# Second batch of a fused attention and SwiGLU kernel: its last q and weight transposes moved from TensorE to DMA, and the third batch's loads and projection moved to fit

## Chip, cores, metric

One NeuronCore of a Trainium2 chip. The metric is device time in microseconds (us) of one execution, median of several. Each changed kernel is timed in the same rounds as the kernel before. A ratio and its 95% interval are from fast runs alone; they are not quite the ratio of the medians quoted beside them. A second measure is used below, the *stream*: from the first TensorE transpose of slot 12 (at 33.8 to 35.2 us, before any TensorE work that the change touches) to the end of the profiled execution. That slot is reached up to 1.4 us earlier or later from run to run, and the stream leaves that out. Each stream is that of one profiled execution.

## The reference

Attention with keys and values projected from 1024 rows to 64 (Linformer), eight batches of eight heads, then a SwiGLU block over all 8192 tokens:

```python
k_proj = einsum('ks,bhsd->bhkd', E, k);  v_proj = einsum('ks,bhsd->bhkd', F, v)
attn = softmax(q @ k_proj.T / sqrt(64));  x = attn @ v_proj       # per batch and head
g = x @ w_gate;  out = (silu(g) * (x @ w_val)) @ w_out            # 512 -> 1536 -> 512
```

## The kernel before

The SwiGLU matmuls of 16 half batches (12 steps each, t = 0 to 191) form one long stream on TensorE. In a step, the g matmuls multiply by `w_gate`, the v matmuls by `w_val`, the y matmuls by `w_out`. Attention for the next batch is cut into small units and dropped into numbered slots of that stream: slot 2t follows the g matmuls of step t, slot 2t+1 follows its v and y matmuls. Elsewhere v is the values of attention, and a *turn* is a transpose of q or of the attention weights, by TensorE or by DMA; the prediction also calls a step a turn. Batches are counted from b = 0, so b = 1 is "the second batch".

```python
BY_DMA = [(b, ch) for b in range(1, B) for ch in range(CH)][1:]   # all but (1, 0)

def load_k(b, ...):  nc.gpsimd.dma_start(out=kb[b]..., in_=k[b]...)   # fp32 -> bf16, from GpSimd's queue
# load_v, load_q(b, ch): the same

def u_KV(b, what="kv"):      # projection: 8 x (k matmul, v matmul), side by side in the array
    for j in range(NJ):
        for _, lo, w, src in todo: nc.tensor.matmul(...)              # L147
    ...                      # evictions, k on ScalarE, v on VectorE

def u_T(b, u):               # turn of q on TensorE: 4 transposes, 1 eviction
def u_A(b, u):               # turn of the attention weights on TensorE: 4 transposes, 1 eviction
def u_TD(b, ch):             # turn of a half batch of q by DMA, from SyncE's queue
    nc.sync.dma_start_transpose(out=t[:], in_=qb[b, ch]...)
def u_AD(b, ch):             # turn of a half batch of weights by DMA, same queue (also used by the stores)
    nc.sync.dma_start_transpose(out=t[:]..., in_=AA.pop((b, ch, "d"))...)

def u_S(b, u): ...           # score: 4 matmuls (L227), exp on ScalarE
def u_R(b, u): ...           # row sum and reciprocal on VectorE
def u_N(b, u): ...           # multiply on GpSimd (L258)
def u_PV(b, ch, pr): ...     # weights x values (L285), eviction to xT, which the SwiGLU matmuls read
```

GpSimd issues the loads and does the multiplies in one queue, in order; SyncE issues DMA turns and stores in one queue, in order.

The softmax here doesn't subtract the row's maximum and nothing guards it: scores larger than these inputs give would overflow.

## Time and profile before

| | kernel before |
|---|---|
| time, median (range) | 573.73 us (572.9 to 574.41, 4 runs) |
| profiled span | 572.4 us |
| TensorE busy | 561.2 us, 98% |
| stream (slot 12 to the end) | 537.75 us |
| TensorE waits after 26 us | none |

Here is the top of the list of TensorE's waits (who waited for whom: us in total, times, longest), all of them in the first 26 us while the first inputs come in:

```profile
PE kvp L147 <- DMA kb<-in_k_dram: 1.3, 2, 1.0
PE warm L458 <- DVE zeros L434: 1.2, 1, 1.2
PE kvp L147 <- DMA vb<-in_v_dram: 1.0, 2, 0.6
```

### The profile page before, as it was taken

The page shows a single profiled execution, that of the slowest core. Times are in us where ns is not written, and L with a number is a line of the kernel's source. Part 1 is how long each engine was busy: PE and PEld are TensorE (multiplying, and loading weights), DVE is VectorE, ACT ScalarE, POOL GpSimd, SP SyncE. Part 2 cuts the span into 40 slices and gives each one's busy share as a digit, 9 for nine tenths or more (in the row PEclk, how much of TensorE's full clock was granted, in tenths as well). Part 3 has the DMA queues.
Part 4 walks back from the last instruction along what each step waited for, and adds up shares of the span by engine and source line. Part 5 has one row for each costly group of instructions (what it writes and reads, how often), then busy time and mean ns, then how long its engine had stood idle before and what let it go on. Part 6 is the DMA issues. An engine that isn't in the chain of part 4 may idle for free.

```text
span 572.4 us, 7867 instructions
## 1 busy us (share of the span) xinstructions
PE 561.2 (98%) x2910; PEld 268.6 (47%) x2967; DVE 336.8 (59%) x580; ACT 237.0 (41%) x416; POOL 107.9 (19%) x121
## 2 busy tenths in 40 slices
PE   8899999999999999999999999999999999999997
PEld 4654544444444444444444444444444444444444
DVE  2787566666466744766556665567546674554550
ACT  1655444353425434444335434354342543443232
POOL 6734131234002400124001330023200220000000
PEclk9999999999999999999999999999999999999999
DMA  9999993539901698037951399204990124100012
GB/s 160 196 200 206 201 161 74 93 64 196 201 37 41 110 190 157 18 75 129 187 108 38 59 179 195 63 22 88 197 176 37 42 52 74 38 37 25 31 39 92
DMA packets 105927, 61.34 MB, mean 107 GB/s; under 512 B 58016, under 2 KB 97696, under 8 KB 105888
## 3 DMA queue, kind: packets, MB, share of 16 engines
q0 software_dynamic: 42288, 29.89, 36.1%
q1 hardware_dynamic: 63312, 30.68, 25.1%
q8 instruction: 23, 0.38, 0.3%
q10 hardware_dynamic: 288, 0.26, 0.1%
q14 instruction: 16, 0.13, 0.1%
HBM read 60.29 MB, written 16.78 MB: 135 GB/s over the span
## 4 chain that ended last, share of the span: by engine, by line
PE 94%; DMA 2%; POOL 1%; ACT 1%; issue 1%; DVE 0%; POOLq 0%
PE yps L360 29%; PE vps L322 29%; PE gps L322 29%; PE kvp L147 3%; PE sc L227 2%; DMA vb<-in_v_dram 2%; PE pv L285 2%; PE aTp L274 0%; ACT xT L135 0%; PE qTp L193 0%; POOL kb L88 0%; PE kTp L172 0%; POOL qb L107 0%; ACT th L334 0%; PE pv L300 0%
## 5 line engine op out<-in xcount | busy, mean ns | idle before, releaser
L341 DVE SCALAR_TENSOR_TENSOR s<-th,gps 128x512 f32<-128x512 f32 x192 | 130.5, 680 | 138.0 <-ACT th L334 137.8
L322 PE MATMUL gps<-xT,wg 128*128 128x512 bf16 (+1 forms) x755 | 195.7, 377 | 1.2
L322 PE MATMUL vps<-xT,wv 128*128 128x512 bf16 (+1 forms) x761 | 195.9, 377 | 0.8
L360 PE MATMUL yps<-wo,hT 128*128 128x512 bf16 (+2 forms) x761 | 191.5, 376 | 0.8
L334 ACT ACTIVATE th<-gps 128x512 f32<-128x512 f32 x192 | 114.6, 597 | 162.6 <-PE gps L322 155.1
L346 DVE TENSOR_TENSOR hT<-s,vps 128x512 bf16<-128x512 f32 x192 | 132.0, 688 | 22.1 <-PE vps L322 1.5
L360 PEld LDWEIGHTS <-hT 128*128 128x128 bf16 x780 | 76.2, 98 | 89.9
L258 POOL TENSOR_TENSOR AAd<-ee,rr 128x512 bf16<-128x512 f32 x52 | 54.1, 1040 | 319.5 <-issue 168.4
L322 PEld LDWEIGHTS <-wv 128*128 128x128 bf16 x776 | 73.9, 98 | 82.9 <-issue 3.3
L322 PEld LDWEIGHTS <-wg 128*128 128x128 bf16 x776 | 74.0, 98 | 81.3 <-issue 0.6
L370 ACT ACTIVATE ysb<-yps 128x512 f32<-128x512 f32 (+1 forms) x65 | 38.4, 590 | 78.1 <-PE yps L360 74.4
L135 ACT CAST xT<-pv 128x512 bf16<-128x512 f32 x62 | 36.1, 585 | 51.3 <-PE pv L285 50.3
L242 DVE TENSOR_REDUCE zz<-ee 128x8 f32<-128x512 f32 x64 | 43.5, 679 | 17.9 <-ACT ee L231 17.9
L231 ACT ACTIVATE ee<-sc 128x512 f32<-128x512 f32 x64 | 37.9, 595 | 17.4 <-PE sc L227 17.4
L285 PE MATMUL pv<-AT,BDV 128*128 128x512 bf16 x60 | 22.6, 379 | 0.1
L227 PEld LDWEIGHTS <-qTd 128*128 128x128 bf16 x208 | 16.0, 98 | 12.3
L227 PE MATMUL sc<-BD,qTd 128*128 128x128 bf16 x208 | 20.1, 219 | 0.1
L135 DVE CAST BDV<-kvp 64x256 bf16<-64x256 f32 x14 | 6.0, 426 | 22.1 <-ACT ks L157 19.1
L258 POOL TENSOR_TENSOR AA<-ee,rr 128x512 bf16<-128x512 f32 x10 | 10.3, 1038 | 35.2 <-DVE rr L244 33.6
L147 PE MATMUL kvp<-kb,ET 128*64 128x512 bf16 (+1 forms) x72 | 15.5, 357 | 1.3 <-DMA kb<-in_k_dram 1.3
L244 DVE RECIPROCAL rr<-zz 128x8 f32<-128x8 f32 x64 | 13.0, 203 | 6.2
L147 PE MATMUL kvp<-vb,FT 128*64 128x512 bf16 (+1 forms) x72 | 15.5, 358 | 1.0 <-DMA vb<-in_v_dram 1.0
(49 smaller groups left out, 144.8 us busy)
## 6 DMA issues: line engine op xcount, KB each, us to landing
out_dram<-ysb SPq DMA_DIRECT2D x63, 256.0 KB, 2.3
qb<-in_q_dram POOLq DMA_DIRECT2D x15, 512.0 KB, 16.6
kb<-in_k_dram POOLq DMA_DIRECT2D x7, 1024.0 KB, 11.6
vb<-in_v_dram POOLq DMA_DIRECT2D x7, 1024.0 KB, 14.2
wo<-in_moe_w_out_dram POOLq DMA_DIRECT2D x2, 768.0 KB, 14.8
wg<-in_moe_w_gate_dram POOLq DMA_DIRECT2D x5, 256.0 KB, 10.4
wv<-in_moe_w_val_dram POOLq DMA_DIRECT2D x5, 256.0 KB, 10.4
kb<-in_k_dram POOLq DMA_DIRECT2D x2, 512.0 KB, 8.7
```

What stands on the lines that cost most here:

```text
L135: (nc.scalar.copy if eng is nc.scalar else eng.tensor_copy)(out=out, in_=in_)
L147: nc.tensor.matmul(out=t[lo : lo + 64, h0:h1].rearrange("p h d -> p (h d)"), lhsT=w[:, j, :], rhs=src[b][:, h0:h1, j, :], start=(j == 0), ...
L227: nc.tensor.matmul(out=ps[:, n, :], lhsT=t[:, n, :], rhs=BD[b % 2][:, 4 * g + n, :], start=True, stop=True)
L231: nc.scalar.activation(out=e[:].rearrange("p h j k -> p (h j k)"), in_=ps[:].rearrange("p a k -> p (a k)"), func=AF.Exp, scale=scale,)
L242: nc.vector.reduce_sum(out=z[:], in_=e[:], axis=AX.X)
L258: eng.tensor_tensor(out=a.rearrange("p j h k -> p h j k"), in0=ee.pop((b, u))[:], in1=rr.pop((b, u))[:].unsqueeze(3).to_broadcast([P, 4, 2 ...
L322: nc.tensor.matmul(out=ps[:, ts], lhsT=(wg, wv)[w][:, kt, f * P : (f + 1) * P], rhs=x[:, kt, ts], start=(kt == 0), stop=(kt == NKT - 1),)
L334: nc.scalar.activation(out=th[:], in_=ps[:], func=AF.Tanh, scale=0.5)
L341: nc.vector.scalar_tensor_tensor(out=s1[:], in0=th[:], scalar=1.0, in1=g[:], op0=ALU.add, op1=ALU.mult)
L346: nc.vector.tensor_tensor(out=hT[c][:, f, :], in0=s1[:], in1=ps[:], op=ALU.mult)
L360: nc.tensor.matmul(out=yy[c][:, cs], lhsT=hT[c][:, f, i * P : (i + 1) * P], rhs=wo[:, f, cs], start=(f == 0), stop=(f == NFT - 1),)
L370: nc.scalar.activation(out=ysb[:, cs], in_=yy[c][:, cs], func=AF.Copy, scale=0.5)
```

## The change

Intent: the half batch (1, 0) is the only one after the first batch whose q and weights are still turned on TensorE. Turn it by DMA like the others. Its q must then be loaded and its k projected earlier, its scores must come at once so that the weights' turn is done in time, and the third batch's loads are put behind all this so that they don't slow the turn. The third batch's projection and scores move to later slots. The diff is cut to its core: equal branches are written out for the batch they serve, old values stand as remarks, and lines without a sign are unchanged.

```diff
-BY_DMA = [(b, ch) for b in range(1, B) for ch in range(CH)][1:]
+BY_DMA = [(b, ch) for b in range(1, B) for ch in range(CH)]
 ... place(b), b == 1:
+            put(22, u_TD, 1, 0)
+            put(29, u_KV, 1, "k")                      # was 34
+            put(32, u_KT, 1)                           # was 36
             put(40, u_KV, 1, "v")
+            sa = (35, 36, 37, 38, 43, 44, 45, 47)      # was (37, 38, 39, 40, 48, 50, 52, 54)
+            put(41, u_AD, 1, 0)
             put(30, u_TD, 1, 1)
+            put(50, u_AD, 1, 1)                        # was 57
+            sp = (44, 45, 46, 46, 66, 67, 68, 69)      # was (43, 44, 45, 46, 66, ...)
-            tt, ta: four u_T and four u_A of (1, 0), slots 35 to 38 and 41 to 44
 ... b == 2 (b > 2 as before):
+            put(s0 + 8, u_KV, b)                       # was s0; s0 = 48
+            put(s0 + 11, u_KT, b)                      # was s0 + 3
+            o = 13                                     # was 14; scores at s0 + o + 3 * j
+            put(s0 + 9, u_TD, b, 0);  put(s0 + 11, u_TD, b, 1)    # were s0 + 3, s0 + 5
 ... load order at the start: weights,
+        load_q(1, 0);  load_k(1)
         load_wo(0);  load_wo(1)                        # q(1, 0) was loaded at slot 20, k(1) after these
 ... loads of the third and fourth batch:
+            at = (46, 47, 48, 48) if b == 2 else ...   # k, v, q, q; were 36, 38, 40, 42
+            s0 = 96 - 20 for b == 3                    # was 96 - 24
```

More of the change, by code (lines that the diff above doesn't have):

```diff
@@ L392, in place @@
         if b == 1:
-            put(30, u_TD, 1, 1)
-            put(34, u_KV, 1, "k")
-            put(36, u_KT, 1)
-            put(40, u_KV, 1, "v")
-            sa = (37, 38, 39, 40, 48, 50, 52, 54)
-            tt = (35, 36, 37, 38)
-            ta = (41, 42, 43, 44)
-            put(57, u_AD, 1, 1)
-            sp = (43, 44, 45, 46, 66, 67, 68, 69)
-        else:
-            put(s0, u_KV, b)
-            put(s0 + 3, u_KT, b)
-            o = 14 if b == 2 else 6
-            put(s0 + (3 if b == 2 else -6), u_TD, b, 0)
-            put(s0 + (5 if b == 2 else -4), u_TD, b, 1)
+            put(22, u_TD, 1, 0)
+            put(29, u_KV, 1, "k")
+            put(32, u_KT, 1)
+            put(40, u_KV, 1, "v")
+            sa = (35, 36, 37, 38, 43, 44, 45, 47)
+            put(41, u_AD, 1, 0)
+            put(30, u_TD, 1, 1)
+            put(50, u_AD, 1, 1)
+            sp = (44, 45, 46, 46, 66, 67, 68, 69)
+        else:
+            put(s0 + (8 if b == 2 else 0), u_KV, b)
+            put(s0 + (11 if b == 2 else 3), u_KT, b)
+            o = 13 if b == 2 else 6
+            put(s0 + (9 if b == 2 else -6), u_TD, b, 0)
+            put(s0 + (11 if b == 2 else -4), u_TD, b, 1)
             sa = [s0 + o + 3 * j for j in range(NJ)]
@@ L412, in place @@
         for j in range(NJ):
-            if (b, j // 4) not in BY_DMA:
-                put(tt[j], u_T, b, j)
-                put(ta[j], u_A, b, j)
             put(sa[j], u_S, b, j)
@@ L507 @@
         load_w_gv(10, 12)
+        load_q(1, 0)
+        load_k(1)
         load_wo(0)
         load_wo(1)
-        load_k(1)
         warm(1)
@@ L532 @@
         put(23, u_PV, 0, 1, 3)
-        put(20, load_q, 1, 0)
         put(20, load_v, 1)
@@ L538 @@
         for b in range(2, B):
-            s0 = 48 * (b - 1) - (12 if b == 2 else 24)
-            put(s0, load_k, b)
-            put(s0 + 2, load_v, b)
-            put(s0 + 4, load_q, b, 0)
-            put(s0 + 6, load_q, b, 1)
+            s0 = 48 * (b - 1) - (20 if b == 3 else 24)
+            at = (46, 47, 48, 48) if b == 2 else (s0, s0 + 2, s0 + 4, s0 + 6)
+            put(at[0], load_k, b)
+            put(at[1], load_v, b)
+            put(at[2], load_q, b, 0)
+            put(at[3], load_q, b, 1)
         for s in slots:
```

## The prediction

> **What bounds the kernel now.** I read the page's first two parts first, then the waits of TensorE, then its timeline around the second batch, then the queues of GpSimd and SyncE over the first 220 us.
>
> ```profile
> PE 561.2 (98%) x2910; PEld 268.6 (47%) x2967; DVE 336.8 (59%) x580; ACT 237.0 (41%) x416; POOL 107.9 (19%) x121
> ...
> PEclk9999999999999999999999999999999999999999
> DMA  9999993539901698037951399204990124100012
> GB/s 160 196 200 206 201 161 74 93 64 196 201 37 41 110 190 157 18 75 129 187 108 38 59 179 195 63 22 88 197 176 37 42 52 74 38 37 25 31 39 92
> ```
>
> TensorE is busy 98% of 572.4 us. Its list of waits holds under 6 us in all, every one before 26 us; asked for 26 to 572 us, the list is empty. So from 26 us on the kernel is one unbroken stream of matmuls, and two rules follow: a matmul taken away shortens the end by its pace, and a new wait of TensorE lengthens it in full, with nothing later to absorb it. The GB/s row (slices of 14.3 us) shows the loads running in plateaus near 200 GB/s with quiet gaps; the three slices from 86 to 129 us are quiet (74, 93, 64 GB/s), because the loads of the third batch (b = 2) lie before them, the last issued at 79.7 us and landed 6.6 us later.
>
> ```profile
> 63.08 0.39 PE L193 MATMUL qTp<-ident_bf,qb 128*128 128x128 bf16 x4
> 63.30 1.03 PE L322 MATMUL gps<-xT,wg 128*128 128x512 bf16 x3
> ```
>
> This is one turn as the change removes it: four transposes of 128 columns start at 63.08 and the next matmul starts at 63.30. A turn costs the stream 0.22 us, 55 ns a transpose; the 219 ns that the source line gives for one is its length in the pipe, not its pace. The four-part turn of the attention weights (L274, 75.77 to 76.00) costs the same.
>
> **What the Trainium skill says.** "TensorE: Matmul & The Clock Gate", section "Back-to-back issue gap", gives about 56 ns for an isolated gap at N = 128 and 81 ns in a stream with weight loads. The trace has 55 ns with weight loads, so I use 55. "DMA: Bandwidth & Descriptors", section "Issuing engines are not separate DMA queues", says that DMAs from SyncE and GpSimd run on the same 16 engines and interleave. The trace agrees: the DMA turn of the weights landed in 4.3 us in the quiet stretch at 103 us, and in 17.2 us beside the loads at 126 us. The same page, section "Measured (HBM→SBUF, 128 partitions, SWDGE, issued from GpSimd)", has 6.15 us for 1 MB. The trace disagrees for these casting loads: the 1024 KB load of k took 10.6 to 11.6 us, so I use the trace. "TensorE: Matmul & The Clock Gate", section "What's actually happening", says that an idle window of about 3.4 us halves TensorE's clock. No idle that long exists here after the start, so the trace cannot say; it only widens my upper end.
>
> **What the change removes.** The second batch's first half loses its four turns of q and four of the weights: 8 x 0.22 us = 1.76 us of the stream, plus eight evictions (four on ScalarE at 0.585 us, four on VectorE at about 0.42 us), which lie beside TensorE and are worth nothing by themselves. All of these are inside 62 to 82 us. The end comes 1.76 us earlier, if no new wait appears. Everything else keeps its count.
>
> **What it moves, and whether it waits.** I place the changed schedule on the old clock: two slots are one (g, v, y) turn of 2.59 us plus what attention puts in.
>
> Early loads: q(1,0) now goes before the two wo loads. The old wo loads, issued at 28.6 and 31.3 us, landed at about 43 and 47; put behind 1.5 MB more, at 200 GB/s, they land near 50.5 and 54.5, some 2.5 us later with the new DMA turn of 0.5 MB between. They are needed at about 59 and 61.5. k(1) lands before 50 and is needed at 53.4. No wait.
>
> First half by DMA: q turned long before slot 35 (63 us). Scores at 63 to 67.5 us, last multiply on GpSimd by about 71.5 (exp 0.6, sum and reciprocal 0.9 behind VectorE's product of the same turn, multiply 1.04). The DMA turn then takes 4.3 to 5.4 us, as the loads that used to fill 62 to 78 us are gone: about 77, needed at slot 44, near 79.5. No wait, 2.5 us to spare. ScalarE in slots 43 to 47 has four exps, four xT evictions, two tanh and two y evictions, some 7.1 us in 7.6; laid out one by one it is never late for a PSUM buffer.
>
> Third batch: this is where I expect a wait. Its loads wait for slots 46 to 48, and GpSimd's queue is in order, so the load of k stands behind the multiply of the score at slot 44. In before the same pattern shows for the fourth batch:
>
> ```profile
> 121.20 1.04 POOL L258 TENSOR_TENSOR AAd<-ee,rr 128x512 bf16<-128x512 f32 x1 [3.97 <-DVE rr L244]
> 122.18 0.94 POOL L88 DMA_DIRECT2D kb<-in_k_dram  x1
> ...
> 126.28 0.94 POOL L97 DMA_DIRECT2D vb<-in_v_dram  x1
> ...
> 130.84 1.81 POOL L107 DMA_DIRECT2D qb<-in_q_dram  x2
> ```
>
> and how long they took to land (columns: count, KB each, us from issue to landing):
>
> ```profile
> kb<-in_k_dram POOLq DMA_DIRECT2D x1, 1024.0 KB, 11.6
> ...
> vb<-in_v_dram POOLq DMA_DIRECT2D x1, 1024.0 KB, 14.2
> AT<-AAd SPq DMA_TRANSPOSE x1, 17.2
> ...
> qb<-in_q_dram POOLq DMA_DIRECT2D x2, 512.0 KB, 16.1
> ```
>
> From k's issue to v's landing is 126.28 + 14.2 - 122.18 = 18.3 us there, and 18 to 19 us in three later batches; those batches had 24 slots (34 us) from load to use. The change leaves 10.
>
> Reckoned: the turn t = 24 began at 87.03 in before. Minus 1.76 removed, plus four scores moved ahead of it (0.88): 86.15. Slot 44's score then is at 79.4, its multiply ends near 84 (5 us after a score starts is what the old trace has there: 67.75 to 72.15, 70.79 to 77.0). So k goes at 84, v behind the next multiply at 86, the q halves at 87 and 88. u_KV(2) at slot 56 falls at 86.15 + 4 x 2.59 + 0.86 = 97.4, and its second matmul already reads v. By v's own 13.2 to 14.4 us, and up to 2 us more because v now follows k by 2 us and not 4 to 5, it lands at 99.3 to 102.5. TensorE waits 2 to 5 us, say 3.5.
>
> Then q(2,0): 16.1 to 18.6 us in the old trace, so 103 to 105.6; its DMA turn 4.9 to 6.2 us, so 108 to 112. The first score, slot 61, would be at 97.4 + 1.85 (projection) + 1.72 + 2.59 + 0.24 + 2.59 = 106.4 without any wait. So the q turn asks for 1.6 to 5.4 us. The two waits don't add: the later start of the projection uses up the second. The larger of them: about 4.0 us.
>
> Later batches: their loads start at slot 76, not 72, for use at 96; 20 slots are 28 us, against 19 needed. No wait. Sum: 574.05 - 1.76 + 4.0 = 576.3 us.
>
> **Rivals.** (a) No new wait: the full 1.76 us is kept, 572.3. For it: the DMA is otherwise quieter there (one store and one turn beside the loads), and whoever placed slots 56 and 61 may have had room. Against: no load of v in steady state landed in under 13.2 us, and the change gives it 11.3. (b) Only one of the two waits, or half of each: a wash, about 574. (c) The wait is a little over 3.4 us and the clock drops for a window: 2 to 3 us more, about 579. (d) The early reordering makes wo late, or the weights' DMA turn misses slot 44: 1 to 3 us more. The spare of 2.5 to 5 us speaks against it. VectorE, ScalarE and GpSimd lose work or keep it; none becomes the bound.
>
> **Range and chances.** The gain is fixed within 0.1 us; the range is the wait's, 0.3 to 7 us: 572.6 to 579.5. Slower by over 2% (585.5) needs 13 us of wait, three times my estimate: 4%. Faster by over 2% (562.6) would need six times what was removed: 1%.
>
> **What would show it.** Right: 32 fewer matmuls on L193 and L274 together; new lines in TensorE's waits, the projection (L147) for the load of v at about 97 to 101 us, the score (L227) for qTd near 107 to 111, together about 4 us, and none elsewhere. The issue of k at 83 to 85 us tests the GpSimd step; v's landing after 99 tests the load step. Wrong: no TensorE wait after 26 us, or v landed by 97 us (then 572.3), or a wait at 55 to 62 us for wo or at 79 us for AT.

## The result, and the profile after

| | before | after |
|---|---|---|
| time, median (range) | 573.73 us (572.9 to 574.41) | 578.35 us (577.16 to 578.76, 4 runs) |
| ratio, 95% interval | | 1.0078 [1.0057, 1.0098] |
| stream | 537.75 us | 542.66 us |
| TensorE waits after 26 us | none | one, 4.5 us |

The change costs 4.6 us, 0.8%; the interval leaves equality out. The page's lines that answer to those of before:

```profile
PE 566.2 (98%) x2935; PEld 267.4 (46%) x2935; DVE 335.2 (58%) x576; ACT 235.1 (41%) x412; POOL 108.0 (19%) x121
...
PEclk9999999899999999999999999999999999999999
DMA  9999839919950599027961299413991023010002
GB/s 172 195 200 197 149 65 187 180 45 152 196 109 19 101 182 191 19 47 126 180 141 38 55 155 198 68 38 76 183 196 38 33 61 74 36 38 19 37 37 92
```

TensorE's busy time and matmul count can't be compared: the trace before has 2910 matmuls to 2967 weight loads, so 57 records are missing, and the gaps that they leave count as idle. The lines of transposes, L193 and L274, have 32 records each where they had 48, as intended. PEclk is the granted clock, the share of full speed at which TensorE was allowed to run: in the eighth slice, 101 to 115 us, it is below 9 tenths. In the GB/s row the quiet slices from 86 to 129 us are gone; now 72 to 87 us (65 GB/s) and 115 to 130 us (45) are quiet. TensorE's waits after 26 us are now a list of one line:

```profile
PE kvp L147 <- DMA vb<-in_v_dram: 4.5, 1, 4.5
```

Slot 37 shows the saving. Before, a score and a turn stand ahead of the g matmuls, after, only a score (0.45 us and 0.23 us):

```profile
66.44 0.39 PE L227 MATMUL sc<-BD,qT 128*128 128x128 bf16 x4
66.66 0.39 PE L193 MATMUL qTp<-ident_bf,qb 128*128 128x128 bf16 x4
66.89 1.03 PE L322 MATMUL gps<-xT,wg 128*128 128x512 bf16 x4
...
65.83 0.39 PE L227 MATMUL sc<-BD,qTd 128*128 128x128 bf16 x4
66.06 1.03 PE L322 MATMUL gps<-xT,wg 128*128 128x512 bf16 x4
```

GpSimd's timeline shows the issue of the third batch's loads, behind the multiplies of the scores at slots 43 and 44 (start, length, engine, line):

```profile
82.43 1.04 POOL L258 TENSOR_TENSOR AAd<-ee,rr 128x512 bf16<-128x512 f32 x1 [1.20 <-DVE rr L244]
83.41 0.94 POOL L88 DMA_DIRECT2D kb<-in_k_dram  x1
84.37 1.06 POOL L258 TENSOR_TENSOR AAd<-ee,rr 128x512 bf16<-128x512 f32 x1
85.36 0.94 POOL L97 DMA_DIRECT2D vb<-in_v_dram  x1
86.30 1.76 POOL L107 DMA_DIRECT2D qb<-in_q_dram  x2
```

These loads and the DMA turn of weights issued at 89.2 us beside them, from issue to landing:

```profile
vb<-in_v_dram POOLq DMA_DIRECT2D x1, 1024.0 KB, 16.4
qb<-in_q_dram POOLq DMA_DIRECT2D x2, 512.0 KB, 21.2
...
AT<-AAd SPq DMA_TRANSPOSE x1, 16.4
```

So v lands at 85.36 + 16.4 = 101.8 us. TensorE's own timeline:

```profile
96.84 0.40 PE L147 MATMUL kvp<-kb,ET 128*64 128x512 bf16 x1
101.78 0.38 PE L147 MATMUL kvp<-vb,FT 128*64 128x512 bf16 x1 [4.54 <-DMA vb<-in_v_dram]
...
103.59 0.63 PE L147 MATMUL kvp<-vb,FT 128*64 128x512 bf16 x1
...
104.58 1.70 PE L322 MATMUL vps<-xT,wv 128*128 128x512 bf16 x4
106.11 1.03 PE L360 MATMUL yps<-wo,hT 128*128 128x512 bf16 x4
```

The first k matmul runs, the first v matmul waits 4.54 us, and then the matmuls take 0.63 us and not 0.38, and four of them take 1.53 us (104.58 to 106.11) and not 0.87. The table by stretches gives the reason; the column behind POOL's is the granted clock:

```profile
99.00:101.00 2.00, 0.00 (x0) 0.00 (x0) 0.00 (x0) 0.00 (x0) 0.00 (x0) 1.00 1.32 181
101.00:103.00 2.00, 1.22 (x10) 0.79 (x11) 0.00 (x0) 0.00 (x0) 0.00 (x0) 0.89 1.37 172
103.00:105.00 2.00, 2.00 (x10) 0.56 (x6) 0.00 (x0) 0.32 (x1) 0.00 (x0) 0.50 1.33 195
105.00:107.00 2.00, 2.00 (x9) 0.85 (x8) 1.57 (x4) 0.26 (x1) 0.00 (x0) 0.76 1.35 235
```

The clock was halved for 3.41 us, from 102.5 to 106.0 us, after the wait, when TensorE was at work again.

The loss adds up. Projection and following v matmuls would take 1.85 + 0.87 us from 96.84, so to 99.56; they end at 106.11, 6.55 us late. Of these 4.70 us are the pause (96.84 + 0.24 to 101.78) and 1.85 us the slow clock (half of 3.41 us is 1.71; the rest of 0.14 us is not explained). Less the 1.76 us predicted for the eight turns, the stream should be 4.8 us longer; it is 4.9.

### The profile page after: what moved, and what is told of

Its sections match the earlier page's. It is cut to its first block, busy times and chain, and to the rows that moved or that the text cites. A ratio compares the mean times of both kernels' runs of the same rounds, so it can differ in the third digit from the quotient of the medians.

```text
span 576.7 us, 7859 instructions
## 1 busy us (share of the span) xinstructions
PE 566.2 (98%) x2935; PEld 267.4 (46%) x2935; DVE 335.2 (58%) x576; ACT 235.1 (41%) x412; POOL 108.0 (19%) x121
## 4 chain that ended last, share of the span: by engine, by line
PE 92%; DMA 4%; DVE 1%; ACT 1%; POOL 0%; issue 0%; SPq 0%; DVEq 0%; POOLq 0%; ACTq 0%
PE vps L322 28%; PE yps L360 28%; PE gps L322 28%; PE kvp L147 3%; DMA vb<-in_v_dram 3%; PE sc L227 2%; PE pv L285 2%; PE warm L455 1%; DMA Fraw<-in_F_dram 1%; DVE zz L242 0%; ACT xT L135 0%; PE kTp L172 0%; POOL AAd L258 0%; PE aTp L274 0%; PE qTp L193 0%
## 5 line engine op out<-in xcount | busy, mean ns | idle before, releaser
L322 PE MATMUL gps<-xT,wg 128*128 128x512 bf16 (+1 forms) x776 | 198.0, 377 | 0.2
L322 PE MATMUL vps<-xT,wv 128*128 128x512 bf16 (+1 forms) x776 | 198.2, 378 | 0.0
L360 PE MATMUL yps<-wo,hT 128*128 128x512 bf16 (+1 forms) x780 | 194.5, 376 | 0.0
L258 POOL TENSOR_TENSOR AAd<-ee,rr 128x512 bf16<-128x512 f32 x56 | 58.3, 1042 | 350.1 <-issue 194.4
L227 PEld LDWEIGHTS <-qTd 128*128 128x128 bf16 x224 | 17.2, 98 | 13.2
L227 PE MATMUL sc<-BD,qTd 128*128 128x128 bf16 x224 | 21.6, 219 | 0.0
L147 PE MATMUL kvp<-vb,FT 128*64 128x512 bf16 (+1 forms) x72 | 16.5, 374 | 4.5 <-DMA vb<-in_v_dram 4.5
L147 PE MATMUL kvp<-kb,ET 128*64 128x512 bf16 (+1 forms) x72 | 16.5, 372 | 0.0
L107 POOL DMA_DIRECT2D qb<-in_q_dram x17 | 15.1, 887 | 0.5 <-DMA wv<-in_moe_w_val_dram 0.5
```

The costliest lines, as they stand in the source:

```text
L147: nc.tensor.matmul(out=t[lo : lo + 64, h0:h1].rearrange("p h d -> p (h d)"), lhsT=w[:, j, :], rhs=src[b][:, h0:h1, j, :], start=(j == 0), ...
L227: nc.tensor.matmul(out=ps[:, n, :], lhsT=t[:, n, :], rhs=BD[b % 2][:, 4 * g + n, :], start=True, stop=True)
L258: eng.tensor_tensor(out=a.rearrange("p j h k -> p h j k"), in0=ee.pop((b, u))[:], in1=rr.pop((b, u))[:].unsqueeze(3).to_broadcast([P, 4, 2 ...
L322: nc.tensor.matmul(out=ps[:, ts], lhsT=(wg, wv)[w][:, kt, f * P : (f + 1) * P], rhs=x[:, kt, ts], start=(kt == 0), stop=(kt == NKT - 1),)
L360: nc.tensor.matmul(out=yy[c][:, cs], lhsT=hT[c][:, f, i * P : (i + 1) * P], rhs=wo[:, f, cs], start=(f == 0), stop=(f == NFT - 1),)
```

## Experiments

Theory: the loss is a deadline missed by the loads of v and q, which stand behind multiplies in GpSimd's queue and are wanted 10 slots later, plus the clock that falls after a pause of that length. Rivals: the DMA turns slow the loads wherever they are put; the later slots of the loads were needless; the slow matmuls come from DMA traffic and not from the pause; only v was late and not q.

In the table, *pause* is the time by which the waiting instruction came late against the pace of the stream, *added* is the time of added matmuls at their pace, and *rest* is stream - 536.08 (the stream of the two versions without a wait, the last two rows) - pause - added.

| run | median us | ratio [95%] | stream | TensorE waits for | pause | added | rest |
|---|---|---|---|---|---|---|---|
| after | 578.35 | 1.0078 [1.0057, 1.0098] | 542.66 | v | 4.70 | 0 | 1.9 |
| loads at 42 | 579.37 | 1.0095 [1.0081, 1.0109] | 543.76 | weights' turn | 4.88 | 0 | 2.8 |
| loads at 36 | 582.67 | 1.0158 [1.0144, 1.0172] | 547.40 | weights' turn | 9.65 | 0 | 1.7 |
| scores later | 579.58 | 1.0108 [1.0093, 1.0123] | 544.43 | weights' turn | 5.39 | 0 | 3.0 |
| fill | 577.02 | 1.0064 [1.0052, 1.0077] | 541.56 | q's turn | 0.77 | 4.75 | 0.0 |
| split projection | 580.71 | 1.0128 [1.0113, 1.0144] | 545.62 | q's turn | 4.78 | 1.84 | 2.9 |
| score at 40 | 571.89 | 0.9988 [0.9972, 1.0004] | 536.08 | nothing | 0 | 0 | 0 |
| use later | 572.61 | 0.998 [0.9963, 0.9997] | 536.08 | nothing | 0 | 0 | 0 |

The median before was 573.53 in the rounds of the first four experiments and 573.21 in those of the last three. All edits below are against the changed kernel, and all results were correct. The rest agrees with the clock in the traces: the time that TensorE worked at half clock, halved, is 1.7, 2.8, 1.7, 3.0 and 2.8 us for after, loads at 42, loads at 36, scores later and split projection. The half clock lasted 3.41 us in after, 10.24 us with the loads at 36, and 6.83 us in the other three.

**Loads at slot 42**

```diff
-            at = (46, 47, 48, 48) if b == 2 else ...
+            at = (42, 43, 44, 44) if b == 2 else ...
```

> The changed kernel with nothing but the third batch's loads brought forward from slots 46, 47, 48, 48 to 42, 43, 44, 44, that is ahead of the multiply of the score of slot 43 in GpSimd's queue. Theory (the loads stand behind multiplies and come too late for the projection at slot 56): the issue of k moves from 83.4 to about 71.6 us, v lands before 92, TensorE waits for nothing after 26 us, the clock stays at 1.00, and the time is 573.7 - 1.8 = 572.0 us, ratio to before 0.997. Rival (the DMA turns themselves slow the loads, whenever they are): v still lands after 97 or the turn of the weights at 71.7 us is slowed and the projection of values waits at 79 us; time above 574.

k went out at 71.8 us and v landed at 93.4 (72.7 + 20.7), in time, as the theory said. But a new wait took the place of the old one:

```profile
PE pv L285 <- DMA AT<-AAd: 4.7, 1, 4.7
```

The weights' turn, issued at 71.88 us, 0.1 us behind k, landed after 12.2 us, where the changed kernel's landed after 4.2 (first line below: the changed kernel):

```profile
AT<-AAd SPq DMA_TRANSPOSE x1, 4.2
...
AT<-AAd SPq DMA_TRANSPOSE x1, 12.2
```

The expectation of 572.0 failed, and the rival's answer came true in its second half: loads beside the turn slow it, even where it is issued with them and not behind them. The loads were slowed as well: k took 16.5 us and v 20.7, where the same loads one behind the other, without that turn, take 11.5 and 16.8 (the version with the score at slot 40, below). So there are two deadlines: the turn at 79 us and v at 97 us.

**Loads at slot 36, as in the kernel before**

```diff
+            at = (36, 38, 40, 42) if b == 2 else ...
```

> The changed kernel with the third batch's loads where the kernel before had them: slots 36, 38, 40, 42. Theory (loads beside a DMA turn slow the turn): k goes out at about 46 us, v at about 68.5, the q halves at about 72, so that the weights' turn issued at 71.7 us takes 12 to 17 us in place of 4.2, and TensorE waits 5 to 10 us for it at slot 44, near 79 us, and then runs at half clock for a window: 577 to 584 us. Rival (moving the loads late was needless): no wait, 572.0.

```profile
PE pv L285 <- DMA AT<-AAd: 9.5, 1, 9.5
```

The turn took 17.0 us, and the time, 582.67, is in the range expected. Its own packets, of 256 bytes, moved only from 77 us on, behind two stores that SyncE had issued before it. From 83 to 84 us the loads (q0) and the turn (q1) had as many packets each (queue: packets, MB, share of the engines):

```profile
q0 software_dynamic: 238, 0.12, 87.8%
q1 hardware_dynamic: 239, 0.06, 46.3%
```

In the changed kernel, with no load beside it, the same turn had 835 packets from 73 to 74 us. So the turn lost most of its pace while packets of the loads moved between its own. This is not all: with the loads at 42 it had only 376 packets from 73 to 74 us, when no packet of a load moved yet; why is open. This is what the later loads of the change were for: left where they were, they would cost 4 us more than the change does. Moving them was right; they were moved too far for the slots in which they are used.

**Scores of the second half later**

```diff
-            sa = (35, 36, 37, 38, 43, 44, 45, 47)
+            sa = (35, 36, 37, 38, 48, 50, 52, 54)
-            put(50, u_AD, 1, 1)
+            put(57, u_AD, 1, 1)
```

> The changed kernel with its loads left at slots 46 to 48, but the scores of the second batch's second half put at slots 48, 50, 52, 54 as in the kernel before (their DMA turn at 57). No multiply then stands between the first half's last one and the loads in GpSimd's queue. Theory (it is the order in GpSimd's queue that holds the loads, not the slot number): the loads go out at about 71.6 us although their slots are unchanged, no wait of TensorE, 572.0 us, ratio 0.997. Rival (the slot sets the time of issue): k goes out at 83 us, v lands at 101, the wait of 4.5 us and the slow clock stay, 578.

```profile
71.04 1.04 POOL L258 TENSOR_TENSOR AAd<-ee,rr 128x512 bf16<-128x512 f32 x1 [1.06 <-ACT ysb L370]
72.02 0.94 POOL L88 DMA_DIRECT2D kb<-in_k_dram  x1
```

The step was right: with the slots of the loads unchanged, k went out at 72.0 us and not at 83.4, because no multiply stood before it. The slot number of a DMA issue is only its place in the queue of its engine. The total was wrong for the reason just found: the loads now fell on the weights' turn (12.3 us, wait 5.2 us).

**TensorE kept busy while v lands**

```diff
+            put(56, warm, 22, "a")          # ahead of u_KV(2) in slot 56: 22 matmuls of zeros
```

> The changed kernel with 22 matmuls of zeros (128x512, results unused) put just ahead of the third batch's projection, at 216 ns each 4.75 us, so that TensorE is busy while v lands. Theory (of the 4.6 us lost over before, 1.8 is the clock that was cut to a half after the idle 4.5 us): the wait for v shrinks to under 0.5 us, the granted clock stays at 1.00 from 97 to 107 us, and the time falls by 1.8 us to about 576.6, although work was added. Rival (the slow matmuls at 102 to 106 us come from the DMA traffic, or zeros do not count as work): slow matmuls stay, 578.3 or more.

The zeros ran from 97.15 to 101.99 us (4.84 us), the wait for v disappeared and the clock stayed whole in every stretch; one of them:

```profile
104.00:106.00 2.00, 2.00 (x10) 0.87 (x9) 1.39 (x3) 0.55 (x1) 0.00 (x0) 1.00 1.29 250
```

The DMA was as busy there (1.29) as in the changed kernel, so the slow matmuls don't come from traffic: they go when TensorE's pause goes. The stream is 1.1 us shorter than after, although 22 matmuls were added, and not the 1.8 expected. The difference is for the most part a new wait of 0.6 us (0.77 us against the pace):

```profile
PE sc L227 <- DMA qTd<-qb: 0.6, 1, 0.6
```

With the slow clock gone the first score is due earlier, and q's turn is next in line: it landed at 111.8 us.

**Projection of the third batch split**

```diff
-            put(s0 + (8 if b == 2 else 0), u_KV, b)
+            put(56, u_KV, 2, "k");  put(63, u_KV, 2, "v")      # b == 2
```

> The changed kernel with the third batch's projection cut in two: that of k at slot 56, that of v at slot 63 (each 8 matmuls alone, 1.84 us, where both together took 1.85 us, so 1.84 us of added work). Theory (the q turn asks for a wait of its own, hidden behind the wait for v): no wait for v, but the first score of the batch at slot 61 is ready at about 106 and waits for the DMA turn of q, which lands at about 111: 4 to 5.5 us of wait on L227, then a window at half clock; 573.7 - 1.8 + 1.8 + 5 + 1.8 = 580.5 us. Rival (only v was late): no wait at all after 26 us and 573.7 us.

```profile
PE sc L227 <- DMA qTd<-qb: 4.6, 1, 4.6
```

580.71 us against 580.5 expected. With v out of the way, q's turn asks for a wait as long as v's: the changed kernel missed two deadlines and paid for one, because the wait for the first put off the second.

**Fifth score at slot 40, loads right behind its multiply**

```diff
-            sa = (35, 36, 37, 38, 43, 44, 45, 47)
+            sa = (35, 36, 37, 38, 40, 44, 45, 47)
+            at = (42, 42, 43, 43) if b == 2 else ...
```

> The changed kernel with the fifth score of the second batch at slot 40 in place of 43 and the third batch's loads right behind its multiply, at slots 42, 42, 43, 43. The multiply then ends near 77 us, which keeps the loads off the weights' DMA turn (71.7 to 76 us) and still sends k out at about 77 and not 83.4. Theory (the change is paid for by two DMA deadlines, 79 us for the weights' turn and 97 us for v, and loads begun between 76 and 78 us meet both): the turn lands in 4.2 us, v lands at 94 to 96, no wait of TensorE after 26 us, clock 1.00, 573.6 - 1.8 = 571.8 us, ratio 0.997. Rival (loads and turns of 3 MB and more can't be fitted into this stretch in any order): a wait of over 1 us stays somewhere, time over 573.

```profile
76.05 1.04 POOL L258 TENSOR_TENSOR AAd<-ee,rr 128x512 bf16<-128x512 f32 x1 [4.42 <-DVE rr L244]
77.04 0.94 POOL L88 DMA_DIRECT2D kb<-in_k_dram  x1
...
vb<-in_v_dram POOLq DMA_DIRECT2D x1, 1024.0 KB, 16.8
```

The multiply of that score, which waits for VectorE, starts just as the weights' turn has landed (71.66 + 4.3 = 76.0 us), so it holds the loads back for 1.1 us more and no longer. That the times meet is a matter of the slot chosen; nothing ties the loads to the turn. v lands at 77.97 + 16.8 = 94.8, wanted at 96.83. TensorE waits for nothing after 26 us. The stream is 536.08 us, 1.67 less than before.

**Loads as changed, use six slots later**

```diff
+            put(s0 + (14 if b == 2 else 0), u_KV, b)           # was 8
+            put(s0 + (16 if b == 2 else 3), u_KT, b)           # was 11
+            o, d = (18, 2) if b == 2 else (6, 3)               # was 13, every third slot
```

> The changed kernel with loads and turns where they are, but the third batch's projection 6 slots later (62), its transposes at 64, its scores from slot 66 every second slot (before: from 61 every third). Theory (the loss is only that v and q are wanted too soon): v lands at 101 and is wanted at 104, q's turn lands at 111 and is wanted at 112; no wait, clock 1.00, 571.8 us, ratio 0.997. Rival: the late scores push the weights' turn of the third batch into the fourth batch's loads, it takes 12 us and more, and TensorE waits for it at slot 87; time 574 or more.

No wait, clock 1.00, stream 536.08 us again: the two ways to meet the deadlines give the same stream to 0.02 us. What the rival feared did come about, as the turn of the second half of the third batch's weights took 14.7 us beside the fourth batch's loads, but it brought no wait.

Against the kernel before, this version is faster by 0.2%, with an interval that just leaves out equality. The interval of the version with the score at slot 40 includes it. By their streams both versions are faster than both kernels, but the gain, 1.67 us, is smaller than the spread of whole runs (572.7 to 574.7 us before, 570.5 to 573.1 with the use later).

## Why the prediction was right, and where it was off

The predicted path held, but for one sign of it that didn't show, and the time lies in the range, but the size was short: the sum adds 2.2 us to 574.05, and the change cost 4.6 us between the medians. That 576.3 is only 2 us from 578.35 owes a little to the start, 574.05 where the median before is 573.73.

- *The saving, 1.76 us.* Held: 1.67 us in both versions without a wait.
- *The early part makes no wait.* Held: no wait between 26 and 96 us. The weights' turn was issued at 71.67 us (about 71.5 foretold) and landed in 4.2; the first product that needs it ran at 79.04 (79.5 foretold).
- *k stands behind the multiply of slot 44's score, issue near 84.* Held: 83.41 us.
- *v lands at 99.3 to 102.5, wait 2 to 5 us, "say 3.5".* Inside the range, but near its top: 101.8 and a pause of 4.70 us. The term taken from the old trace, 13.2 to 14.4 us plus up to 2, came out at 16.4 (the prediction's two landings are 0.1 us later than its own sum from an issue at 86). That v was issued 2 us behind k, and not 4 to 5 us, is the likely cause; no run tests it alone.
- *q's turn lands at 108 to 112; the two waits don't add.* The times held: it landed at 111.1 (106.62 + 4.5), before the first score at 112.48, while the split projection showed that alone it costs a pause of 4.78 us. But the prediction also named a line of L227 waiting for q's turn as a sign, and none appeared: the wait for v and the slow clock put off the first score past the landing. In the fill, without the slow clock, that line came, with 0.6 us. The load of q was under-sized (20.3 us for the first half, 21.2 for the median of both, against 16.1 to 18.6).
- *The sum, 4.0 us of wait.* This is the term that was mis-sized: TensorE lost 6.55 us, 4.70 us of pause and 1.85 us of slow clock. The halved clock had been named only as rival (c), for a wait "a little over 3.4 us", and was not put into the centre although the reckoned wait of 4.0 was already over that. The kernel with matmuls of zeros in the gap showed this term by itself: slow clock gone, 1.9 us of rest down to 0.

The rival of a wait for wo (d) did not come: the two wo loads, issued at 31.7 and 33.0, took 19.7 and 23.3 us, so both had landed by 56.4 (54.5 foretold), and were wanted at 58.5 and 61. Rival (a) failed for the change as it stands, and is what the last two versions do.

What the prediction did not see is how narrow the way out is. It blamed the late loads, and the obvious mend, earlier loads, was slower than the change itself: a turn issued 0.1 us behind the first load took 12.2 us. The first experiment's expectation had no term for this and left it to its rival.

## What to carry to other kernels

Where the bounding engine has no waits, removing work from it is worth that work and no more, while any new wait counts in full, and if it is long (4.5 us and more here) the slow clock behind it added 1.7 to 3.0 us. Before moving a load, list who wants it and when, and count the lead from the moment at which the queue of its issuer reaches it, behind which instruction it stands, not from its place in the program. A DMA turn with a deadline wants a stretch without loads (4.2 us here, and 12.2 to 17.0 us beside them): hold the loads back with an instruction that their queue has to do anyway, and move what uses them if they then come late.

## What the Trainium skill lacked or had wrong

- "TensorE: Matmul & The Clock Gate", "What's actually happening": half clock after an idle window of about 3.4 us. The runs agree (0.50 after pauses of 4.7 us and more; none after 0.8 us). The section doesn't say how many such windows a pause brings: after 4.70 us the half clock lasted 3.41 us, after 4.8 to 5.4 us it lasted 6.83 us, after 9.65 us 10.24 us. It cost 1.7 to 3.0 us, least after the longest pause, as most of that slow time was spent idle. Nor does it say whether matmuls of zeros count as work: they kept the clock at 1.00.
- "DMA: Bandwidth & Descriptors", "Measured (HBM→SBUF, 128 partitions, SWDGE, issued from GpSimd)": 1 MB in 6.15 us. It has no figure for loads that cast. Those here, to 1 MB of bf16, took 10.6 to 11.7 us for k and 12.1 to 16.4 us for v behind it (the kernel before from its fourth batch on, the changed one from its third), and 16.5 to 16.9 and 20.7 to 21.6 us beside the weights' turn with the loads at 42 and the scores later. These are from issue to landing, with the issue in it, which the page's figure leaves out.
- The same page, "Rules for kernel authors", says that a transpose next to ordinary DMAs needs nothing. That is so for its result (all runs were correct). No page says what the loads beside it cost in time: the weights' turn at 72 us took 4.2 to 4.3 us without loads (512 KB), and 12.2 to 17.0 us beside loads from GpSimd, even if issued with the first of them.
- "TensorE: Matmul & The Clock Gate", "Back-to-back issue gap": 81 ns for N = 128 in a stream with weight loads. The transposes here paced at 55 ns, and eight turns of four were worth 1.67 us, 52 ns each.
